# A hand-ordered attention and maxout kernel: its first part and its loop get new orders of loads, fillers, products and stores

## The chip, the cores and the metric

The kernel runs on one core of one Trainium2 chip. The metric is the device time of one execution in microseconds (us). Of the kernel before there are three timed runs and one profiled execution, and all numbers below are from those. Engines are called as in the profile: PE (TensorE), PEld (its weight loads), DVE (VectorE), ACT (ScalarE), POOL (GpSimd), SP (SyncE).

## What is computed

Eight batches of eight heads. For each head, `x` is 512 x 64 and `state` is 32 x 64:

```
a     = softmax(x @ state^T / 8)            # 512 x 32
xread = a @ state                           # 512 x 64
a2    = softmax(state @ x^T / 8)            # 32 x 512
sread = a2 @ x                              # 32 x 64
tok   = heads of [xread; sread] side by side  # (8 * 544) x 512
h     = max(tok @ w1, tok @ w2, tok @ w3)   # 4352 x 768
out   = h @ w_out                           # 4352 x 512, float32
```

## The kernel before, in words

Everything is fed to TensorE as bf16. The kernel never forms `xread`: since `xread @ W = a @ (state @ W)`, it first computes for each batch `G = state @ W`, a tile of 128 x 2 x 3 x 768 (`g_slice`, line 371, makes one slice of 128 columns of all three W; `g_run`, line 384, makes a run of up to 512 columns), and then the first layer is `aT` times `G` (`layer1`, line 417: 128 columns of the hidden layer for 512 tokens, three products of two matmuls each, one PSUM bank per product). The maximum of the three is taken in three steps: `max_first` (line 427, ACT copies the first product out of PSUM), `max_second` (line 432, DVE) and `max_third` (line 437, DVE, which writes `ht`). `layer2` (line 441) multiplies `ht` by `w_out`, six matmuls for one quarter of the batch's tokens, and `layer2_out` copies the result into `osb`, which is stored from there.

The attention weights `aT` take a chain of their own: `x` is transposed (`x_turn`, line 230, on PE for batches 0 and 1, by halves of the heads; `x_turn_dma`, line 246, by a transposing DMA on SP's queue for the others), `scores` (line 253, PE), `exps` (line 267, ACT), `sums` (line 272, DVE), `weights` (line 279, POOL or DVE) and a second transposition (`a_turn` on PE, `a_turn_dma` on SP's queue). The states are cast (`states_cast`), turned on PE (`states_turn`) and placed as a block diagonal (`states_place`). The state reads are small products (`sread`, line 314), scaled by DVE; `pad` (line 305) has POOL prepare a copy of `x` with ones for them from batch 2 on; their transposing DMA is `srt`, and `ap` puts the result in its place.

The order of the work is written out by hand, as three strings of short operations: FIRST (line 18) does batches 0 and 1 up to their hidden layers and starts batch 2; EACH (line 40) is performed for b = 2 to 6, its numbers being relative to b; LAST (line 48) ends the work. An operation such as `gc 1 0 A` names batch 1, slice 0 and the engine (A, D, P, S for ACT, DVE, POOL, SP). Every engine executes its own operations in the order of the text; semaphores hold an operation until its inputs are there and its buffer is free. Which of four single PSUM banks, or two pairs of banks, an operation gets is written out in the strings BANKS and PAIRS in the same order.

Loads of `x` (`lxg` for half of the heads of one batch, `lx` for all of them), of W (`lw m0 m1 i`: slices m0 to m1-1 of 128 columns of w1, w2 or w3 for i = 0, 1, 2) and of `w_out` (`lwo`) convert float32 to bf16 on their way and are issued by POOL into one queue, in order. The first half of batch 0 comes as float32 on SP's queue (`lxu`) and is cast by DVE (`cxu`). The states (`lst`) come by ACT's or SP's queue.

`busy n` (line 207) issues n matmuls of zeros; they compute nothing and are called fillers below. In FIRST there are 30 of them, all ahead of the first `layer1`.

Of the kernel before, what the change touches and what calls it, by code (L numbers as in the profile page):

```python
# [15 lines left out]


FIRST = """
    lxu 0 0 S; lst 0 A; lxg 1 0; zero; warm; clr 0; clr 1; clr 2; clr 3; stc 0 D; ident; busy 1;
    lst 1 S; busy 2; busy 1; busy 2; busy 1; busy 1; stt 0; busy 1; busy 2; cxu 0 0 D; stp 0 AD;  # L20
    stc 1 A; lxg 0 1; xt 0 0; lxg 1 1; lw 0 1 0; busy 1; lw 0 3 1; xtc 0 0 A; xt 1 0; xones 0; busy 2;
    busy 1; lw 0 2 2; xtc 1 0 DA; sc 0 0; xt 0 1; lw 1 2 0; busy 1; busy 1; lw 2 4 0; lw 2 4 2; sc 1 0;
    ex 0 0; ex 1 0; busy 1; xtc 0 1 A; xt 1 1; busy 1; busy 1; sum 0 0; busy 1; stt 1; lw 3 6 1; busy 1;
    sc 0 1; busy 1; ex 0 1; xtc 1 1 D; busy 1; sc 1 1; ex 1 1; busy 1; stp 1 A; lxg 2 1; wt 0 0 P;
    busy 1; xones 1; at 0 0; sum 1 0; busy 1; busy 1; sum 0 1; sr 0; busy 1; sum 1 1; g 0 0; wt 1 0 P;
    g 1 0; gc 1 0 A; wt 0 1 D; sr 1; busy 1; srs 0; lxg 2 0; at 0 1; at 1 0; wt 1 1 P; atc 0 0 D;
    at 1 1; gc 0 0 D; atc 0 1 A; lw 4 6 2; srs 1; atc 1 0 A; g 1 1; atc 1 1 D; gc 1 1 A; g 0 1;
    l1 0 0 1; g 1 2; m0 0 0; g 0 2; l1 1 0; gc 0 1 D; gc 1 2 A; l1 1 1; m0 1 0; ma 0 0; mb 0 0; ma 1 0;
    lw 4 6 0; mb 1 0; l1 0 1; g 0 3; m0 1 1; g 1 3; gc 0 2 A; l1 0 2; ma 1 1; l1 1 2; xtd 2; pad 2;
    m0 0 1; mb 1 1; ma 0 1; m0 0 2; lst 3 A; gc 0 3 DA; l1 0 3; m0 1 2; lwo; gc 1 3 A; ones; g 0 5;  # L30
    g 1 4; mb 0 1; ma 0 2; lxg 3 0; m0 0 3; mb 0 2; gc 0 5 A; lst 2 S; ma 1 2; l1 1 3; stc 3 P; m0 1 3;
    l1 0 5; mb 1 2; g 0 4; gc 1 4 A; g 1 5; ma 0 3; l1 1 4; m0 0 5; gc 0 4 A; mb 0 3; ma 1 3; m0 1 4;
    lxg 3 1; l1 0 4; sc 2 -; gc 1 5 A; xtd 3; mb 1 3; gr 2 1024 1280; m0 0 4; gr 2 1280 1792; ex 2 -;
    grc 2 1280 1792 A; l1 1 5; m0 1 5; ma 0 5; stc 2 A; mb 0 5; gr 2 512 1024; gr 2 1792 2304; sr 2;
    ma 1 4; mb 1 4; ma 0 4; mb 0 4; l2 0 3; grc 2 512 1024 A; stt 2; grc 2 1024 1280 D; gr 2 0 512;
    l2 0 0; l2 0 1; l2 0 2; grc 2 1792 2304 A; sum 2 -; l2c 0 0 A; grc 2 0 512 A; ma 1 5; wt 2 - P;
    srs 2; l2c 0 3 A; stp 2 A; mb 1 5; l2c 0 2 D; atd 2; so 0 2 4 P; stt 3; l2c 0 1 A; stp 3 DA;
    so 0 0 2 A; lx 4;
"""
EACH = """  # L40
    gr 1 0 512; gr 1 1792 2304; l2 -1 0; grc 1 0 512 D; l1 0 0; pad 1; srt -2; m0 0 0; sc 1 -; l2 -1 1;
    grc 1 1792 2304 A; ma 0 0; l2 -1 3; ex 1 -; gr 1 1024 1280; gr 1 512 1024; l2c -1 0 D;
    gr 1 1280 1792; sr 1; l2c -1 1 A; so -1 0 2 P; mb 0 0; l1 0 1; grc 1 1024 1280 A; l2c -1 3 A; xtd 2;
    m0 0 1; l1 0 2; m0 0 2; l1 0 3; sum 1 -; srs 1; grc 1 1280 1792 DA; ma 0 1; l1 0 5; mb 0 1; m0 0 3;
    ma 0 2; ap -2 A; wt 1 - P; mb 0 2; m0 0 5; l2 -1 2; ma 0 3; grc 1 512 1024 A; mb 0 3; l1 0 4;
    ma 0 5; mb 0 5; l2c -1 2 D; atd 1; m0 0 4; so -1 2 4 P; ma 0 4; lx 3; mb 0 4;
"""
LAST = """
    srt 6; l1 7 0; srt 7; l2 6 0; l1 7 2; m0 7 0; l1 7 3; l1 7 4; ap 7 D; m0 7 2; srt 5; ap 6 A; ma 7 0;
# [14 lines left out]
"""  # L64

BANKS = """
# [3 lines left out]
"""  # L70
PAIRS = """
    0110101010 1010101010 1001010010 1001010010 10
"""


# [601 lines left out]
```

## Time and profile before

| what | value |
|---|---|
| timed runs | 153.05, 153.10, 153.87 us (median 153.1) |
| profiled execution, its own time | 153.01 us |
| span of that profile | 151.2 us |
| PE busy | 146.6 us (97%) |
| DVE busy | 115.1 us (76%) |
| ACT busy | 85.4 us (56%) |
| POOL busy | 54.7 us (36%) |
| first row of `layer1` | starts 16.56 us from the span's start |

The span is the time between the first and the last instruction that the profile shows; the execution is 1.8 us longer. Busy time is counted per engine; the engines work side by side, so the shares don't add up. The chain of waits follows the work that ended last back from the end: at each step to what released it, or to the instruction ahead of it on the same engine. In its listing in order of time, each row has a start, a length, an engine and a line. All times are in us from the start of the span, unless ns is written.

### The profile page before, as it was taken

The page shows a single profiled execution, that of the slowest core. Times are in us where ns is not written, and L with a number is a line of the kernel's source. Part 1 is how long each engine was busy: PE and PEld are TensorE (multiplying, and loading weights), DVE is VectorE, ACT ScalarE, POOL GpSimd, SP SyncE. Part 2 cuts the span into 40 slices and gives each one's busy share as a digit, 9 for nine tenths or more (in the row PEclk, how much of TensorE's full clock was granted, in tenths as well). Part 3 has the DMA queues.
Part 4 walks back from the last instruction along what each step waited for, and adds up shares of the span by engine and source line. Part 5 has one row for each costly group of instructions (what it writes and reads, how often), then busy time and mean ns, then how long its engine had stood idle before and what let it go on. Part 6 is the DMA issues. An engine that isn't in the chain of part 4 may idle for free.

```text
span 151.2 us, 3644 instructions
## 1 busy us (share of the span) xinstructions
PE 146.6 (97%) x1434; PEld 73.6 (49%) x1434; DVE 115.1 (76%) x202; ACT 85.4 (56%) x147; POOL 54.7 (36%) x74
## 2 busy tenths in 40 slices
PE   6999999999999999999999999999999999999992
PEld 2465444344444443444354435443544445679771
DVE  6458899889168799879986998798879887675353
ACT  3567866779677671767175817581758353331220
POOL 6998518301336505460456054604260100001500
PEclk9999999999999999999999999999999999999999
DMA  3999999994919979998199829982133110300545
GB/s 112 241 193 195 198 196 203 161 197 59 204 53 262 225 89 269 152 193 182 60 168 228 174 94 163 206 176 80 72 139 87 68 79 7 131 8 17 188 170 198
DMA packets 38581, 22.30 MB, mean 147 GB/s; under 512 B 22032, under 2 KB 36368, under 8 KB 38560
## 3 DMA queue, kind: packets, MB, share of 16 engines
q0 software_dynamic: 15200, 13.44, 46.6%
q1 hardware_dynamic: 21920, 6.95, 23.5%
q10 hardware_dynamic: 1440, 1.64, 3.2%
q8 instruction: 12, 0.20, 0.5%
q14 instruction: 9, 0.07, 0.2%
HBM read 15.20 MB, written 8.91 MB: 159 GB/s over the span
## 4 chain that ended last, share of the span: by engine, by line
PE 92%; DMA 4%; issue 1%; POOL 1%; DVE 1%; POOLq 0%
PE pw L415 47%; PE po L446 25%; PE pg L362 6%; PE po L461 4%; DMA x<-in_x_dram 4%; PE psr L326 2%; PE ps L261 2%; PE idle L210 2%; PE pgh L362 1%; PE pat L294 1%; POOL x L169 1%; DVE held L521 0%; PE pt L221 0%; PE pxt L236 0%; PE idle L519 0%
## 5 line engine op out<-in xcount | busy, mean ns | idle before, releaser
L415 PE MATMUL pw<-aT,G 128*128 128x512 bf16 x288 | 66.6, 379 | 0.0
L430 ACT CAST t<-pw 128x512 bf16<-128x512 f32 (+1 forms) x54 | 30.4, 563 | 35.3 <-PE pw L415 21.6
L415 PEld LDWEIGHTS <-G 128*128 128x128 bf16 x288 | 27.2, 98 | 33.8 <-issue 2.4
L435 DVE TENSOR_TENSOR t<-t,pw 128x512 bf16<-128x512 bf16 (+1 forms) x54 | 35.3, 653 | 10.2 <-ACT t L430 7.7
L446 PE MATMUL po<-wout,ht 128*128 128x512 bf16 x168 | 39.8, 379 | 0.0
L439 DVE TENSOR_TENSOR ht<-t,pw 128x512 bf16<-128x512 bf16 x48 | 32.9, 685 | 4.1
L476 POOL DMA_DIRECT2D out_dram<-osb x12 | 6.9, 575 | 49.6 <-ACT t L430 20.4
L446 PEld LDWEIGHTS <-ht 128*128 128x128 bf16 x168 | 15.3, 98 | 19.2 <-issue 2.1
L283 POOL TENSOR_TENSOR a<-e,rden 128x1024 bf16<-128x1024 bf16 (+1 forms) x9 | 14.9, 1650 | 10.3 <-DVE rden L277 9.2
L402 ACT CAST G<-pg 128x1024 bf16<-128x1024 f32 (+1 forms) x19 | 17.1, 908 | 0.0
L310 POOL COPY xp<-x 128x1024 bf16<-128x1024 bf16 x12 | 12.3, 1065 | 5.0 <-DMA x<-in_x_dram 5.0
L453 DVE COPY osb<-po 128x512 f32<-128x512 f32 x14 | 9.6, 685 | 5.6 <-PE po L446 5.6
L453 ACT COPY osb<-po 128x512 f32<-128x512 f32 x15 | 8.9, 593 | 5.8 <-PE po L446 5.8
L210 PE MATMUL idle<-zero 128*128 128x512 bf16 x30 | 10.0, 436 | 1.3 <-DVE zero L188 1.3
L275 DVE TENSOR_REDUCE seen<-e 128x32 f32<-128x1024 bf16 (+1 forms) x10 | 10.0, 998 | 1.5 <-ACT e L268 1.5
L362 PE MATMUL pg<-w,bd 64*32 64x512 bf16 (+1 forms) x288 | 10.8, 362 | 0.0
L268 ACT ACTIVATE e<-ps 128x1024 bf16<-128x1024 f32 (+1 forms) x10 | 8.6, 861 | 2.1 <-PE ps L261 2.1
L402 DVE CAST G<-pg 128x1024 bf16<-128x1024 f32 (+1 forms) x10 | 9.5, 947 | 0.0
L471 POOL DMA_DIRECT2D out_dram<-osb x4 | 2.2, 542 | 19.9 <-ACT osb L465 19.9
L380 ACT CAST G<-pg 128x768 bf16<-128x768 f32 (+1 forms) x10 | 7.7, 774 | 2.1 <-PE pg L362 2.1
L415 PE MATMUL pw<-atp,w 128*128 128x256 bf16 x72 | 8.7, 272 | 0.0
L415 PEld LDWEIGHTS <-w 128*128 128x128 bf16 x72 | 6.9, 98 | 1.5
(71 smaller groups left out, 114.3 us busy)
## 6 DMA issues: line engine op xcount, KB each, us to landing
out_dram<-osb POOLq DMA_DIRECT2D x11, 512.0 KB, 3.1
x<-in_x_dram POOLq DMA_DIRECT2D x4, 512.0 KB, 6.6
x<-in_x_dram POOLq DMA_DIRECT2D x7, 256.0 KB, 8.4
w<-in_moe_w_dram POOLq DMA_DIRECT2D x5, 256.0 KB, 8.6
w<-in_moe_w_dram POOLq DMA_DIRECT2D x2, 384.0 KB, 8.8
wout<-in_moe_w_out_dram POOLq DMA_DIRECT2D x1, 768.0 KB, 9.5
out_dram<-osb SPq DMA_DIRECT2D x3, 256.0 KB, 2.3
osb<-in_x_dram SPq DMA_DIRECT2D x1, 512.0 KB, 4.0
```

The lines of the kernel that those rows point to most:

```text
L210: nc.tensor.matmul(p, zero[:, 0:128], zero, start=True, stop=True)
L275: nc.vector.reduce_sum(out=den, in_=parity(e[b], g), axis=AX.X)
L283: times[c](out=parity(a[b], g).rearrange("p j g s n -> p j (g s) n"), in0=parity(e[b], g).rearrange("p j g s n -> p j (g s) n"), in1=rdens ...
L310: nc.gpsimd.tensor_copy(out=xp[b][:, :, :, g * (D + 1):g * (D + 1) + D], in_=v[:, g])
L362: nc.tensor.matmul(p(s, g), bd(b, 2 * s + g)[64 * g:64 * g + 64, g, :], f(w_sb[64 * g:64 * g + 64, s]), start=True, stop=True, tile_positi ...
L402: copier[c[g]](out=v[:, g:h], in_=p[:, g:h, 0:c1 - c0])
L415: nc.tensor.matmul(pw[i][:, 0:n], lhs(i, k), rhs(k), start=(k == 0), stop=(k == nk - 1))
L430: nc.scalar.copy(out=t0s[b, m][:, 0:n], in_=open_ps["l", b, m][0][:, 0:n])
L435: nc.vector.tensor_max(t1s[b, m][:, 0:n], t0s.pop((b, m))[:, 0:n], open_ps["l", b, m][1][:, 0:n])
L439: nc.vector.tensor_max(ht[b][:, m, :], t1s.pop((b, m))[:, 0:n], open_ps.pop(("l", b, m))[2][:, 0:n])
L446: nc.tensor.matmul(p, ht[b][:, m, j * 128:(j + 1) * 128], wout_sb[:, m, :], start=(m == 0), stop=(m == NM - 1))
L453: copier[c[i]](out=o[:, j, i * w:i * w + w], in_=p[:, i * w:i * w + w])
```

## The change

Only the strings FIRST, EACH, BANKS and PAIRS differ; no function does, and LAST is the same text.

In FIRST:

- POOL sets the ones beside `x` first (`xones 0; xones 1`), and its queue then has batch 0's second half, both halves of batch 1, and W in twelve loads instead of nine: slices 0 and 1 of w2, slice 0 of w1, slice 0 and slice 1 of w3, slice 1 of w1, slice 2 of each, and the rest in five larger ones. Batch 2's `x` stands behind all of W (before: ahead of the last two W loads).
- The state loads 1 and 2 move from SP's queue to ACT's, load 1 from the very start to behind `xtc 1 1`; the cast of states 0 moves from DVE to ACT, those of 1 and 2 from ACT to POOL. The turning of states 1 (`stt 1`) moves from the middle of the attention of batch 1 to behind the fifth `layer1`.
- Batch 0's scores, sums and weights of both halves are finished ahead of batch 1's. The layers go `l1 0 0, 0 1, 0 2, 1 0, 1 1, 1 2, 0 3, 1 3, 0 5, 1 4, 0 4, 1 5` (before: `0 0, 1 0, 1 1, 0 1, 0 2, 1 2, 0 3, 1 3, 0 5, 1 4, 0 4, 1 5`).
- `lwo` is issued directly behind batch 2's `x`, and `pad 2`, which waits for that `x` on POOL, comes far later (before: `pad 2` ahead of `lwo`).
- At the end, batch 0's two stores both go by POOL's queue with the load of batch 4 between them (before: one by POOL's ahead of that load, the other by ACT's).
- 24 fillers instead of 30.

In EACH: the second `layer2` of the batch before moves ahead of the first `layer1`, the `g_run`s trade places in pairs, `srt` stands behind `xtd` on SP's queue, `ap` and the first store are last, and three evictions trade engines (`grc 1 1792 2304` from ACT to ACT and DVE, `grc 1 1280 1792` the other way, two `l2c` swap).

```diff
--- before
+++ after
 FIRST = """
-    lxu 0 0 S; lst 0 A; lxg 1 0; zero; warm; clr 0; clr 1; clr 2; clr 3; stc 0 D; ident; busy 1;
-    lst 1 S; busy 2; busy 1; busy 2; busy 1; busy 1; stt 0; busy 1; busy 2; cxu 0 0 D; stp 0 AD;
-    stc 1 A; lxg 0 1; xt 0 0; lxg 1 1; lw 0 1 0; busy 1; lw 0 3 1; xtc 0 0 A; xt 1 0; xones 0; busy 2;
-    busy 1; lw 0 2 2; xtc 1 0 DA; sc 0 0; xt 0 1; lw 1 2 0; busy 1; busy 1; lw 2 4 0; lw 2 4 2; sc 1 0;
-    ex 0 0; ex 1 0; busy 1; xtc 0 1 A; xt 1 1; busy 1; busy 1; sum 0 0; busy 1; stt 1; lw 3 6 1; busy 1;
-    sc 0 1; busy 1; ex 0 1; xtc 1 1 D; busy 1; sc 1 1; ex 1 1; busy 1; stp 1 A; lxg 2 1; wt 0 0 P;
-    busy 1; xones 1; at 0 0; sum 1 0; busy 1; busy 1; sum 0 1; sr 0; busy 1; sum 1 1; g 0 0; wt 1 0 P;
-    g 1 0; gc 1 0 A; wt 0 1 D; sr 1; busy 1; srs 0; lxg 2 0; at 0 1; at 1 0; wt 1 1 P; atc 0 0 D;
-    at 1 1; gc 0 0 D; atc 0 1 A; lw 4 6 2; srs 1; atc 1 0 A; g 1 1; atc 1 1 D; gc 1 1 A; g 0 1;
-    l1 0 0 1; g 1 2; m0 0 0; g 0 2; l1 1 0; gc 0 1 D; gc 1 2 A; l1 1 1; m0 1 0; ma 0 0; mb 0 0; ma 1 0;
-    lw 4 6 0; mb 1 0; l1 0 1; g 0 3; m0 1 1; g 1 3; gc 0 2 A; l1 0 2; ma 1 1; l1 1 2; xtd 2; pad 2;
...
+    lst 0 A; lxu 0 0 S; zero; clr 0; clr 1; clr 2; clr 3; warm; xones 0; busy 1; busy 1; busy 1;
+    xones 1; lxg 0 1; lxg 1 0; busy 1; stc 0 A; busy 1; busy 1; ident; busy 1; busy 1; busy 1;
+    cxu 0 0 D; lxg 1 1; busy 1; stt 0; xt 0 0; busy 1; xtc 0 0 D; lw 0 2 1; busy 1; stp 0 A; xt 0 1;
+    busy 1; lw 0 1 0; sc 0 0; ex 0 0; xt 1 0; busy 1; busy 1; busy 1; lw 0 1 2; lw 1 2 2; busy 1;
+    xtc 0 1 D; xtc 1 0 A; sc 0 1; xt 1 1; busy 1; sum 0 0; wt 0 0 D; ex 0 1; busy 1; busy 1; busy 1;
+    at 0 0; sc 1 0; lw 1 2 0; lw 2 3 2; lw 2 3 1; xtc 1 1 A; lw 2 3 0; busy 1; lst 1 A; ex 1 0; sum 0 1;
+    sum 1 0; busy 1; lw 3 6 2; sc 1 1; sr 0; wt 0 1 P; g 0 0; ex 1 1; g 1 0; wt 1 0 P; sr 1; at 0 1;
+    atc 0 0 A; busy 1; g 1 1; at 1 0; sum 1 1; gc 1 0 A; atc 0 1 D; lw 3 4 0; srs 1; g 0 1; wt 1 1 D;
+    atc 1 0 D; gc 0 0 A; lw 3 6 1; gc 1 1 A; l1 0 0; g 0 2; gc 0 1 A; m0 0 0; g 1 2; at 1 1; lw 4 6 0;
+    gc 0 2 A; lxg 2 1; stc 1 P; l1 0 1; m0 0 1; srs 0; l1 0 2; gc 1 2 A; lxg 2 0; ma 0 0; atc 1 1 D;
+    mb 0 0; l1 1 0; m0 0 2; lst 2 A; xtd 2; ma 0 1; mb 0 1; ma 0 2; l1 1 1; m0 1 0; m0 1 1; lwo; mb 0 2;
+    ma 1 0; g 1 3; g 0 3; stt 1; gc 1 3 A; stc 2 P; mb 1 0; l1 1 2; gc 0 3 A; g 0 4; lxg 3 0; ma 1 1;
...
+    mb 1 3; m0 0 5; ma 0 5; g 1 5; lst 3 A; gr 2 0 512; gc 1 5 A; l1 1 4 1; grc 2 0 512 DA; m0 1 4;
+    mb 0 5; ma 1 4; gr 2 1280 1792; gr 2 512 1024; grc 2 1280 1792 AD; ones; l1 0 4; stt 2; m0 0 4;
+    ma 0 4; mb 0 4; sc 2 -; stc 3 P; xtd 3; pad 2; mb 1 4; l2 0 3; stp 2 AD; l2 0 1; ex 2 -; sum 2 -;
...
 EACH = """
-    gr 1 0 512; gr 1 1792 2304; l2 -1 0; grc 1 0 512 D; l1 0 0; pad 1; srt -2; m0 0 0; sc 1 -; l2 -1 1;
-    grc 1 1792 2304 A; ma 0 0; l2 -1 3; ex 1 -; gr 1 1024 1280; gr 1 512 1024; l2c -1 0 D;
-    gr 1 1280 1792; sr 1; l2c -1 1 A; so -1 0 2 P; mb 0 0; l1 0 1; grc 1 1024 1280 A; l2c -1 3 A; xtd 2;
...
+    pad 1; gr 1 1792 2304; gr 1 0 512; grc 1 1792 2304 AD; l2 -1 0; l2 -1 1; l1 0 0; grc 1 0 512 D;
+    l2c -1 0 A; m0 0 0; sc 1 -; l2 -1 3; gr 1 1024 1280; ex 1 -; xtd 2; gr 1 1280 1792; l2c -1 1 D;
+    ma 0 0; gr 1 512 1024; mb 0 0; sr 1; grc 1 1024 1280 A; l1 0 1; l1 0 2; sum 1 -; l1 0 3; srs 1;
...
+    l1 0 4; so -1 2 4 P; m0 0 4; ma 0 4; lx 3; mb 0 4; atd 1; ap -2 A; so -1 0 2 P;
```

More of the change, by code (lines that the diff above doesn't have):

```diff
@@ L29 @@
-    lw 4 6 0; mb 1 0; l1 0 1; g 0 3; m0 1 1; g 1 3; gc 0 2 A; l1 0 2; ma 1 1; l1 1 2; xtd 2; pad 2;
[L30 to L38, printed above, removed]
+    lst 0 A; lxu 0 0 S; zero; clr 0; clr 1; clr 2; clr 3; warm; xones 0; busy 1; busy 1; busy 1;
@@ new lines @@
+    ma 1 0; g 1 3; g 0 3; stt 1; gc 1 3 A; stc 2 P; mb 1 0; l1 1 2; gc 0 3 A; g 0 4; lxg 3 0; ma 1 1;
+    m0 1 2; mb 1 1; stp 1 DA; ma 1 2; g 0 5; gc 0 5 D; lxg 3 1; mb 1 2; gc 0 4 A; l1 0 3; g 1 4;
+    gr 2 1792 2304; l1 1 3; m0 0 3; gc 1 4 A; m0 1 3; ma 0 3; l1 0 5; mb 0 3; grc 2 1792 2304 A; ma 1 3;
+    mb 1 3; m0 0 5; ma 0 5; g 1 5; lst 3 A; gr 2 0 512; gc 1 5 A; l1 1 4 1; grc 2 0 512 DA; m0 1 4;
+    mb 0 5; ma 1 4; gr 2 1280 1792; gr 2 512 1024; grc 2 1280 1792 AD; ones; l1 0 4; stt 2; m0 0 4;
@@ L39 @@
+    ma 0 4; mb 0 4; sc 2 -; stc 3 P; xtd 3; pad 2; mb 1 4; l2 0 3; stp 2 AD; l2 0 1; ex 2 -; sum 2 -;
+    l1 1 5; stt 3; l2c 0 1 D; l2 0 2; l2c 0 3 A; m0 1 5; ma 1 5; l2c 0 2 D; wt 2 - P; l2 0 0; stp 3 A;
+    mb 1 5; sr 2; gr 2 1024 1280; srs 2; l2c 0 0 D; so 0 0 2 P; lx 4; so 0 2 4 P; grc 2 512 1024 A;
+    atd 2; grc 2 1024 1280 D;
 """
 EACH = """
-    gr 1 0 512; gr 1 1792 2304; l2 -1 0; grc 1 0 512 D; l1 0 0; pad 1; srt -2; m0 0 0; sc 1 -; l2 -1 1;
-    grc 1 1792 2304 A; ma 0 0; l2 -1 3; ex 1 -; gr 1 1024 1280; gr 1 512 1024; l2c -1 0 D;
@@ L43 @@
-    gr 1 1280 1792; sr 1; l2c -1 1 A; so -1 0 2 P; mb 0 0; l1 0 1; grc 1 1024 1280 A; l2c -1 3 A; xtd 2;
-    m0 0 1; l1 0 2; m0 0 2; l1 0 3; sum 1 -; srs 1; grc 1 1280 1792 DA; ma 0 1; l1 0 5; mb 0 1; m0 0 3;
-    ma 0 2; ap -2 A; wt 1 - P; mb 0 2; m0 0 5; l2 -1 2; ma 0 3; grc 1 512 1024 A; mb 0 3; l1 0 4;
-    ma 0 5; mb 0 5; l2c -1 2 D; atd 1; m0 0 4; so -1 2 4 P; ma 0 4; lx 3; mb 0 4;
+    pad 1; gr 1 1792 2304; gr 1 0 512; grc 1 1792 2304 AD; l2 -1 0; l2 -1 1; l1 0 0; grc 1 0 512 D;
+    l2c -1 0 A; m0 0 0; sc 1 -; l2 -1 3; gr 1 1024 1280; ex 1 -; xtd 2; gr 1 1280 1792; l2c -1 1 D;
@@ L47 @@
+    ma 0 0; gr 1 512 1024; mb 0 0; sr 1; grc 1 1024 1280 A; l1 0 1; l1 0 2; sum 1 -; l1 0 3; srs 1;
+    l1 0 5; l2c -1 3 A; m0 0 1; m0 0 2; ma 0 1; mb 0 1; ma 0 2; m0 0 3; mb 0 2; srt -2; ma 0 3;
+    wt 1 - P; m0 0 5; mb 0 3; l2 -1 2; grc 1 1280 1792 A; grc 1 512 1024 A; ma 0 5; mb 0 5; l2c -1 2 D;
+    l1 0 4; so -1 2 4 P; m0 0 4; ma 0 4; lx 3; mb 0 4; atd 1; ap -2 A; so -1 0 2 P;
 """
@@ L66 @@
 BANKS = """
[3 rows of a table removed]
[3 rows of a table added]
 """
 PAIRS = """
-    0110101010 1010101010 1001010010 1001010010 10
+    0110101010 1010101101 0101010101 0101010101 01
 """
```

6 rows, old and new, of the table BANKS are left out of this document.

## The prediction

> **What bounds the kernel now.** First the page: busy time of each engine, and the span in forty slices.
>
> ```profile
> PE 146.6 (97%) x1434; PEld 73.6 (49%) x1434; DVE 115.1 (76%) x202; ACT 85.4 (56%) x147; POOL 54.7 (36%) x74
> ...
> PE   6999999999999999999999999999999999999992
> ```
>
> PE is busy in all slices but the first and the last. Some of it is fillers, so next comes the view of who waited for whom, for PE alone:
>
> ```profile
> PE idle L210 <- DVE zero L188: 1.3, 1, 1.3
> PE idle L519 <- DVE osb L465: 0.4, 1, 0.4
> PE pxt L236 <- DVE x L177: 0.2, 1, 0.2
> ```
>
> Only 0.2 us of waiting lies inside the run. An order of the same products can then gain only where PE does nothing useful, which is the start. Third, the chain of waits in order of time (start, length, what) shows that stretch:
>
> ```profile
> 3.58 5.97 DMA x<-in_x_dram
> ...
> 9.60 0.62 PE pxt L236 x8
> 10.22 0.65 PE idle L210 x3
> 10.87 0.22 PE pt L221 x4
> 11.09 0.22 PE idle L210
> 11.31 0.23 PE ps L261 x8
> 11.54 0.43 PE idle L210 x2
> 11.97 0.23 PE ps L261 x8
> 12.21 0.43 PE idle L210 x2
> 12.64 0.22 PE pat L294 x4
> 12.86 0.43 PE idle L210 x2
> 13.29 0.56 PE psr L326 x32
> 13.85 0.32 PE idle L210
> 14.18 0.45 PE pg L362 x16
> 14.62 0.56 PE psr L326 x32
> 15.19 0.32 PE idle L210
> 15.51 0.67 PE pat L294 x12
> 16.18 0.45 PE pg L362 x16
> 16.63 1.40 PE pw L415 x6
> ...
> 33.35 0.47 PE ps L261 x16
> ...
> 35.82 0.56 PE pg L362 x16
> ```
>
> The chain hangs on the last half of x of batches 0 and 1, which lands at 9.55. From then on PE is never idle, but 12 matmuls behind it are fillers: 0.65 + 0.22 + 3 x 0.43 + 2 x 0.32 = 2.80 us. From 16.63 all is work. So the time is: when the last x lands, plus the fillers and waits behind it, plus work that the change leaves the same (each product of before is in the new text once).
>
> **Fillers behind the last x: -1.3 us.** The new order also turns batch 1's second half (`xt 1 1`) last of the four. Ahead of it PE has done the same in both orders: states 0 turned, three halves turned, two half scores. Behind it the new text has 4 + 2 + 1 = 7 fillers, at 0.65 / 3 = 0.216 us each 1.51 us: 2.80 - 1.51 = 1.29 us less. Ahead of 9.55 stand 30 - 12 = 18 before and 24 - 7 = 17 now; there PE waits for x anyway. Turning states 1 (0.22) and one turning of `a` (0.22) also move behind the first `layer1`; they stay work, so the end gains nothing by them.
>
> The new steps, from rows above: `xt 1 1` 9.60 to 10.22; four fillers 11.08; `at 0 0` 11.30; `sc 1 0` 11.53; two fillers 11.96; `sc 1 1` 12.19; `sr 0` 12.75; `g 0 0` and `g 1 0` 13.20; `sr 1` 13.76; `at 0 1` 13.98, filler and turnover 14.30; `g 1 1`, `at 1 0`, `g 0 1` 14.95; then `l1 0 0`. Do the inputs keep up?
>
> ```profile
> L380 ACT CAST G<-pg 128x768 bf16<-128x768 f32 x9 | 7.3, 806 | 2.1 <-PE pg L362 2.1
> ...
> L283 POOL TENSOR_TENSOR a<-e,rden 128x512 bf16<-128x512 bf16 x3 | 3.4, 1135 | 0.6 <-DVE rden L277 0.6
> ...
> L275 DVE TENSOR_REDUCE seen<-e 128x16 f32<-128x512 bf16 x4 | 2.7, 669 | 1.5 <-ACT e L268 1.5
> ...
> L268 ACT ACTIVATE e<-ps 128x512 bf16<-128x512 f32 x4 | 2.4, 599 | 1.3 <-PE ps L261 1.3
> ...
> L297 ACT COPY aT<-pat 128x512 bf16<-128x512 bf16 x2 | 1.1, 588 | 0.3 <-PE pat L294 0.3
> L277 DVE RECIPROCAL rden<-seen 128x16 f32<-128x16 f32 x4 | 1.0, 253 | 0.1
> ...
> L197 POOL MEMSET x<- 128x64 bf16 x2 | 0.3, 170 | 0.0
> ```
>
> (Columns: count, busy us, mean ns; the lines by form.) The weights of batch 1's first half: 11.53 + 0.60 + 0.67 + 0.25 + 1.14 and a little between, about 14.25, for `at 1 0` at 14.5: in time by a quarter us. `G 0 0`: after `sc 1 1` at 12.19 ACT has an exponential (0.60), `atc 0 0` (0.59), `gc 1 0` (0.81) and `gc 0 0` (0.81), one behind the other, to 15.1: **late by about 0.2 us** for `l1 0 0`. I count +0.2, with bounds 0 and 0.5.
>
> **When the last x lands: -0.1.** Ahead of the x loads POOL now sets ones twice, 0.34 us at most. On the other side, state load 1 (128 KB) no longer runs beside them; at the rate of the next fence that is up to 0.66 us. Bounds -0.66 and +0.34; I take -0.1, near the middle.
>
> **W by slices: 0.** The busy time of each engine in two stretches, with DMA share and GB/s at the end:
>
> ```profile
> 10.00:22.00 12.00, 12.00 (x187) 6.25 (x185) 10.37 (x22) 9.05 (x15) 6.50 (x9) 1.00 1.43 198
> ...
> 44.90:60.15 15.25, 15.25 (x149) 6.82 (x148) 12.62 (x21) 8.86 (x15) 7.05 (x10) 1.00 0.95 210
> ```
>
> At 198 GB/s a load of 256 KB takes 1.32 us. Behind the last x at 9.55 stand `lw 0 2 1` and two single slices for `g 0 0`: 2.65 us, 12.2, wanted 12.75. Two more for `g 1 1`: 13.5, wanted 14.3. Three more for `g 0 2`: 15.5, wanted one `layer1` (1.40) behind 15.1, so 16.5. But a single slice may move slower. Before has one directly behind that x; its issue and its landing:
>
> ```profile
> 4.32 1.58 POOL L180 DMA_DIRECT2D w<-in_moe_w_dram  x2
> ```
>
> ```profile
> w<-in_moe_w_dram POOLq DMA_DIRECT2D x1, 128.0 KB, 6.0
> ```
>
> It lands at 10.32, 0.77 us behind the x, where the rate gives 0.66. With seven at 0.77, `g 0 2` has its slices at 9.55 + 1.32 + 5.39 = 16.26, still 0.2 early. So zero, but with little cover: each 0.1 us more on a slice costs up to 0.7 us less 0.2.
> The Trainium skill, "DMA: Bandwidth & Descriptors", Specifications, puts line rate at 512 B and more for a transfer and says that smaller ones are read, modified and written; a slice of 128 columns writes runs of 256 B. By that rule slices would go well below the rate and the change would lose; the 0.77 us above speaks for a small loss only.
>
> **w_out and batch 2's transposing transfer: 0.** Before, that transfer starts when batch 2's x lands:
>
> ```profile
> 22.13 3.34 SPq L248 DMA_TRANSPOSE xT<-x  x1
> ```
>
> ```profile
> wout<-in_moe_w_out_dram POOLq DMA_DIRECT2D x1, 768.0 KB, 9.5
> xT<-x SPq DMA_TRANSPOSE x1, 8.1
> ```
>
> It lands at 30.2, and its reader, the scores of batch 2 at 33.35, never waits. Now 512 KB of W come ahead of that x: 22.13 + 2.65 = 24.8, and 8.1 us later is 32.9 (33.4 with the slower slices). The scores now have four runs of G (0.28 each by the row at 35.82, which holds two) and one turning (0.22) ahead of them that stood behind: 33.35 - 1.1 + 1.3 = 33.55. So the 3.1 us of cover shrinks to 0.1 to 0.7, and I count nothing. w_out is issued right behind x instead of behind `pad 2`, which waits for that x. From 24.8 it takes 3.97 us at 198 GB/s, or at worst its 9.5 us of before, so it lands between 28.8 and 34.3; the first `layer2` stands behind the scores, at 34.0. I count zero, with 0.3 as the upper bound.
>
> **Banks and evictions: +0.1 in FIRST, 0 in the loop.** Four banks serve all single products, so a late eviction holds PE. Five `layer1` now follow with only one gap; DVE needs two steps of them each. No PE wait is seen before; I take +0.1, bounds 0 and 0.5. A round of the loop is 15.25 us, of which PE fills 15.25 and DVE 12.62. The same products stand in it; the half evictions that change engines go both ways, so no engine's sum moves. The cover is DVE's 2.6 us. Without it each 0.1 us of a round costs 0.5 us in five rounds. The load of batch b+3 keeps its place, and `srt` ahead of `atd` on SP has a whole `layer2` (1.29) more of cover, since the second one now stands ahead of the first `layer1`.
>
> **Sum.** -1.29 + 0.2 - 0.1 + 0.1 = -1.1. The profiled execution took 153.01 us (span 151.2, and 1.8 around it), the median of the runs is 153.1: the forecast is **151.9 us**, own range 151.2 to 152.3. A measurement of this kernel can tell about 0.5%, 0.77 us, from no change.
>
> **Rivals.**
>
> (1) *A slice of W costs as much as two* (1.32 us). For it: half of the run length, and the rule cited. Against it: the 0.77 us. `g 0 0` waits to 13.5 (0.8), `g 1 1` to 16.15 (1.1 more), `g 0 2` to 20.1 (1.8 more): +3.6, **155.5**. The loss at `g 0 2` is 7s - 5.6 us for a cost of s; from s = 0.96 the gain is gone, from 1.07 it is slower by over 0.5%. Half rate: 5%; in between (0.85 to 1.05, 152.3 to 153.5): 12%.
>
> (2) *Batch 2's transposing transfer waits for all of w_out* (3.97 us at 198 GB/s). It lands at 24.8 + 4.0 + 8.1 = 36.9, PE stands at the scores until then: +3.3, **155.2**, slower. It decides from 35.4 on. For it: the cover shrinks to some tenths, and the two already ran side by side with 8.1 and 9.5 us. Against it: before, it also had W and w_out beside it. 12%, half of that for a smaller delay near 153.8.
>
> (3) *The fillers stood for waits that come back*: ACT's row of four steps ends half a us later, or x lands 0.34 later. The gain falls to 0.3 to 0.6: **152.5**. 11%.
>
> (4) *The loop's new places cost 0.2 us in each of five rounds*: +1.0, **152.9**. Against it: unchanged sums of each engine. 5%.
>
> **How the numbers follow.** Forecast 55%, of which a few per cent lie below 151.2 (x early by its bound, no waits: 153.0 - 1.29 - 0.66 = 151.05). Rivals: (1) 17, (2) 12, (3) 11, (4) 5. Faster by over 0.5% (below 152.25) is the forecast and a little of (3): 0.57. Same: (3), (4), most of (1) in between: 0.25. Slower: (2), half rate: 0.18. For 8 in 10 the range runs from 151.0 to 153.8; half rate and the whole of (2) stay out.
>
> **What would show it.** The chain's `pw` row should start near 15.2 instead of 16.63, with seven fillers behind the turning at 9.6. PE's waits should show at most some tenths, at `pw` of batch 0 on ACT's G. A PE wait on a transfer at `pg` before 17 us is (1), at the scores of batch 2 near 33.5 is (2). A round of the loop should still be 15.25 us; if not, (4). The forecast is wrong if the first `pw` starts early and the end doesn't.

## The result: 0.8% slower, and the profile after

The changed kernel takes 1.008 times as long as the kernel before (95% interval 1.0052 to 1.0109), about 1.2 us more; the forecast was 1.1 us less, and the time lies above the range. It took 154.16 to 155.22 us (in run **a_again** 155.13 and 156.11), where before took 153.05 to 153.87; about half of its executions were 4 to 6 us longer still, at a lower granted clock of PE, and the comparisons leave these out. The profile below, from a_again, is of an execution of the unchanged new text that took 155.13 us, with a span of 153.3 us. It is one of the longer ones: against the profile of before it is 2.1 us longer, where the mean difference is 1.2 us. So the parts below are those of this profile and not of the mean.

Busy time, and PE and the DMA engines in forty slices, from its page:

```profile
PE 145.9 (95%) x1428; PEld 73.3 (48%) x1428; DVE 117.9 (77%) x205; ACT 84.5 (55%) x143; POOL 57.2 (37%) x79
...
PE   6789999994999999999999999999999999999992
...
DMA  4999999998635979899379838993603060210455
```

The tenth slice, 34.5 to 38.3 us, has a hole that before didn't have, and from 3.8 to 34.5 us the DMA engines are busy nine tenths or more. PE's waits name it (engine, line, what it waited for; total us, times, longest):

```profile
PE ps L261 <- DMA xT<-x: 2.1, 1, 2.1
...
PE pxt L236 <- DMA x<-in_x_dram: 1.2, 2, 0.9
```

`ps` on `xT` is the scores of batch 2 waiting for its transposing transfer. That one wait is as long as the whole difference of the two spans, 153.3 - 151.2 = 2.1 us. The second new wait, 1.2 instead of 0.2 us, is for `x` at the start. The chain in order of time now hangs on both:

```profile
2.33 6.75 DMA x<-in_x_dram
...
9.12 0.62 PE pxt L236 x8
9.74 0.86 PE idle L210 x4
10.61 0.23 PE ps L261 x8
10.84 0.45 PE pxt L236 x8
...
18.95 7.58 DMA x<-in_x_dram
...
26.55 10.67 DMA xT<-x
...
37.27 0.64 PE ps L261 x16
```

Before, PE itself was the chain from 9.60 us on. Now it runs through batch 2's `x`, which lands at 26.53, then through 10.67 us of the transposing transfer, and only at 37.27 back to PE. The order of time on PE at the start, from its timeline (start, length, engine, line, operation; in brackets the wait ahead of it):

```profile
7.81 0.62 PE L236 MATMUL pxt<-ident,x 128*128 128x128 bf16 x8 [0.94 <-DMA x<-in_x_dram]
9.12 0.62 PE L236 MATMUL pxt<-ident,x 128*128 128x128 bf16 x8 [0.25 <-DMA x<-in_x_dram]
10.68 0.61 PE L236 MATMUL pxt<-ident,x 128*128 128x128 bf16 x8
16.22 1.47 PE L415 MATMUL pw<-aT,G 128*128 128x512 bf16 x6
17.62 0.64 PE L362 MATMUL pg<-w,bd 64*32 64x384 bf16 x16
```

and the same of before, from the last turning on:

```profile
9.60 0.62 PE L236 MATMUL pxt<-ident,x 128*128 128x128 bf16 x8
...
16.56 1.47 PE L415 MATMUL pw<-aT,G 128*128 128x512 bf16 x6
17.96 0.52 PE L362 MATMUL pg<-w,bd 64*32 64x384 bf16 x16
```

So the 2.1 us of the two spans fall into: the last turning starts at 10.68 instead of 9.60 (+1.08); from there to the first `layer1` it is 5.54 instead of 6.96 us (-1.42); the wait at the scores (+2.12); and 0.3 us that are left. The -1.42 us are not all gain: one turning of `a` and the turning of states 1, 0.44 us of work by the rows in the prediction, moved behind the first `layer1` and come back in what is left. Counted so, the start gave nothing in this profile.

### The profile page after: what moved, and what is told of

The parts are those of the page before. It is cut to its first block, busy times and chain, and to the rows that moved or that the text cites. A ratio compares the mean times of both kernels' runs of the same rounds, so it can differ in the third digit from the quotient of the medians.

```text
span 158.8 us, 3616 instructions
## 1 busy us (share of the span) xinstructions
PE 147.2 (93%) x1415; PEld 74.6 (47%) x1428; DVE 117.9 (74%) x205; ACT 84.4 (53%) x143; POOL 57.3 (36%) x79
## 4 chain that ended last, share of the span: by engine, by line
PE 79%; DMA 14%; POOL 3%; issue 1%; DVE 1%; ACT 1%; DVEq 0%
PE pw L415 36%; PE po L446 24%; DMA xT<-x 9%; DMA x<-in_x_dram 6%; PE idle L210 5%; PE po L461 4%; PE pg L362 3%; PE ps L261 3%; PE psr L326 1%; POOL w L180 1%; PE pxt L236 1%; PE pgh L362 1%; POOL a L283 1%; POOL x L169 0%; DVE held L521 0%
## 5 line engine op out<-in xcount | busy, mean ns | idle before, releaser
L430 ACT CAST t<-pw 128x512 bf16<-128x512 f32 (+1 forms) x54 | 30.5, 564 | 29.5 <-PE pw L415 28.7
L415 PEld LDWEIGHTS <-G 128*128 128x128 bf16 x288 | 27.2, 98 | 33.1 <-issue 1.8
L283 POOL TENSOR_TENSOR a<-e,rden 128x1024 bf16<-128x1024 bf16 (+1 forms) x8 | 13.5, 1693 | 19.7 <-ACT osb L453 11.5
L476 POOL DMA_DIRECT2D out_dram<-osb x13 | 7.5, 575 | 32.8 <-ACT t L430 27.1
L402 ACT CAST G<-pg 128x1024 bf16<-128x1024 f32 (+1 forms) x19 | 15.9, 866 | 2.2 <-PE pg L362 2.0
L453 DVE COPY osb<-po 128x512 f32<-128x512 f32 x16 | 11.0, 687 | 4.4 <-PE po L446 4.4
L453 ACT COPY osb<-po 128x512 f32<-128x512 f32 x13 | 7.7, 593 | 9.3 <-PE po L446 9.3
L261 PE MATMUL ps<-bd,xT 128*128 128x64 bf16 x128 | 5.8, 199 | 5.4 <-DMA xT<-x 5.4
L402 DVE CAST G<-pg 128x512 bf16<-128x512 f32 (+1 forms) x12 | 10.5, 906 | 0.2 <-ACT G L402 0.2
L380 ACT CAST G<-pg 128x768 bf16<-128x768 f32 x11 | 8.4, 803 | 2.8 <-PE pg L362 2.7
L210 PE MATMUL idle<-zero 128*128 128x512 bf16 x24 | 8.6, 491 | 1.3 <-DVE zero L188 1.3
L180 POOL DMA_DIRECT2D w<-in_moe_w_dram x12 | 9.1, 772 | 1.1 <-DMA w<-in_moe_w_dram 0.7
L471 POOL DMA_DIRECT2D out_dram<-osb x4 | 2.2, 542 | 19.4 <-ACT osb L465 19.4
```

The source lines that it names most:

```text
L180: nc.gpsimd.dma_start(out=w_sb[:, :, i, m0 * 128:m1 * 128], in_=(moe_w1, moe_w2, moe_w3)[i].rearrange("(kk p) f -> p kk f", p=128)[:, :, m ...
L210: nc.tensor.matmul(p, zero[:, 0:128], zero, start=True, stop=True)
L283: times[c](out=parity(a[b], g).rearrange("p j g s n -> p j (g s) n"), in0=parity(e[b], g).rearrange("p j g s n -> p j (g s) n"), in1=rdens ...
L402: copier[c[g]](out=v[:, g:h], in_=p[:, g:h, 0:c1 - c0])
L415: nc.tensor.matmul(pw[i][:, 0:n], lhs(i, k), rhs(k), start=(k == 0), stop=(k == nk - 1))
L430: nc.scalar.copy(out=t0s[b, m][:, 0:n], in_=open_ps["l", b, m][0][:, 0:n])
```

## The experiments

All times are ratios to the kernel before on the same chip, with 95% intervals. The changed kernel stands at 1.008.

**a_again**: the changed kernel as it is.

> The changed kernel once more, as the base for the others and for a profile that PE's throttle did not disturb. Theory A (the transposing transfer of batch 2 is late, since it now runs beside w_out and batch 3's x, and PE stands at the scores of batch 2): a PE wait on xT of 1 us or more at about 34 us, and about 154.3 to 155 us. Theory B (W by slices is the whole loss): a PE wait at pg near 17 us of 1.2 us, none or only some tenths at the scores. Under both the first layer-one row starts near 15.4.

Its profile is the one above. The wait is at `sc 2`, and none is on W: theory A. The first `layer1` starts at 16.22, where both theories had 15.4, since `x` was late.

**b_wout_first**: the kernel before, with nothing moved but w_out's load.

```diff
-    ... l1 1 2; xtd 2; pad 2;
+    ... l1 1 2; lwo; xtd 2; pad 2;
-    ... m0 1 2; lwo; gc 1 3 A;
+    ... m0 1 2; gc 1 3 A;
```

> The kernel before with one part of the change alone: w_out is issued ahead of the padding of batch 2, so it is in the queue while batch 2's transposing transfer runs. Theory A: that transfer takes over 10 us instead of 8.1 and its 3 us of cover before the scores of batch 2 shrink to about 1 or are gone; 153.1 to 154.5. Theory B or no effect of w_out: it lands 8 us after its issue, 153.1.

1.0072 (1.0049 to 1.0095), 154.56 us. Nothing else of the order is changed (the first `layer1` starts at 16.85, before at 16.56), and this one move costs nearly what the whole change does. Waits, chain and the transfers' own times (size, us from issue to landing):

```profile
PE ps L261 <- DMA xT<-x: 1.2, 1, 1.2
```

```profile
22.22 12.55 DMA xT<-x
...
34.82 0.64 PE ps L261 x16
```

```profile
wout<-in_moe_w_out_dram POOLq DMA_DIRECT2D x1, 768.0 KB, 12.9
```

The transposing transfer is issued at 22.22, as in before (22.13), and takes 12.55 us instead of 8.1. w_out, issued at 17.23, lands at 30.1; the transposing transfer lands 4.6 us behind it, with half of batch 3's `x` (issued at 24.32, landed at 34.2) beside it.

**a_wout_late**: the changed kernel with `pad 2; lwo` in before's order.

```diff
-    ... m0 1 1; lwo; mb 0 2;
+    ... m0 1 1; pad 2; lwo; mb 0 2;
-    ... stc 3 P; xtd 3; pad 2; mb 1 4; ...
+    ... stc 3 P; xtd 3; mb 1 4; ...
```

> The changed kernel with w_out put back behind the padding of batch 2 (which waits for that batch's x), nothing else. Theory A1 (w_out in the queue is what slows the transposing transfer): the transfer lands 8 to 9 us after its issue at 26.5, so PE waits under 1 us at the scores, but w_out now lands 9 us behind 29, so PE waits 1 to 4 us at the first layer two instead: 154 to 157. Theory A2 (batch 3's x, or the late x of batch 2 alone, is what hurts): the transfer still takes over 10 us.

1.0136 (1.0114 to 1.0158), 155.13 us: slower than the changed kernel. The wait at the scores is gone, and another one is there:

```profile
PE po L446 <- DMA wout<-in_moe_w_out_dram: 2.2, 1, 2.2
```

```profile
18.44 7.69 DMA x<-in_x_dram
...
28.16 9.72 DMA wout<-in_moe_w_out_dram
```

```profile
xT<-x SPq DMA_TRANSPOSE x1, 4.4
```

With nothing of POOL's queue ahead of it the transposing transfer takes 4.4 us, where theory A1 had 8 to 9. But w_out now waits for batch 2's `x`, which lands at 26.1, and for `pad 2`, and lands at 37.9; the first `layer2` wants it at 35.7. With that `x` as late as this, one of the two is late in both orders that were tried.

**a_sc_late**: the changed kernel with `sc 2 -` behind two `layer2` of batch 0.

```diff
-    ma 0 4; mb 0 4; sc 2 -; stc 3 P; xtd 3; pad 2; mb 1 4; l2 0 3; stp 2 AD; l2 0 1; ex 2 -; sum 2 -;
+    ma 0 4; mb 0 4; stc 3 P; xtd 3; pad 2; mb 1 4; l2 0 3; stp 2 AD; l2 0 1; sc 2 -; ex 2 -; sum 2 -;
```

> The changed kernel with the scores of batch 2 placed behind two layer-two groups (2.6 us later on PE), nothing else. Theory A: most of the wait on xT is covered, up to 2.6 us come back: 152 to 153 us, and slow executions become rare. Theory B: no change, 154.3.

1.026 (1.0182 to 1.0338): both theories missed. PE no longer waits for `xT`, and yet the time rises. The exponentials and sums of batch 2 stand ahead of evictions on ACT and DVE and now start later, and PE waits for banks:

```profile
PE po L446 <- DVE osb L453: 1.0, 1, 1.0
PE pw L415 <- ACT osb L453: 0.8, 1, 0.8
```

Moving the reader away from the transfer was no free repair here.

**a_x3_late**: the changed kernel with batch 3's `x` behind `pad 2` and its transposing transfer behind `atd 2`.

```diff
-    ... gc 0 3 A; g 0 4; lxg 3 0; ma 1 1;
-    ... gc 0 5 D; lxg 3 1; mb 1 2; ...
+    ... gc 0 3 A; g 0 4; ma 1 1;
+    ... gc 0 5 D; mb 1 2; ...
-    ... stc 3 P; xtd 3; pad 2; mb 1 4; ...
+    ... stc 3 P; pad 2; lxg 3 0; lxg 3 1; mb 1 4; ...
-    atd 2; grc 2 1024 1280 D;
+    atd 2; xtd 3; grc 2 1024 1280 D;
```

> The changed kernel with batch 3's x loaded behind the padding of batch 2, so that only w_out stands beside batch 2's transposing transfer (and batch 3's transposing transfer behind the one of batch 2's weights on SP). Theory A2 (batch 3's x beside the transfer is what spreads it out): the transfer takes about 8 us, the wait at the scores falls under 1 us, slow executions vanish, 153 to 153.8. Theory A1: it still takes 10 us or more and PE waits about 2 us, 154.5.

1.0046 (1.0018 to 1.0074), 153.8 us. The transposing transfer of batch 2 was issued at 27.19 and took

```profile
xT<-x SPq DMA_TRANSPOSE x1, 6.7
```

instead of 10.7, beside the end of w_out and no other load of POOL's (w_out was issued at 20.03 and took 11.1 us). So in the changed kernel both are in its way: w_out, and the 512 KB of batch 3's `x` that POOL issues from 0.14 us behind it on (at 26.69). This profile is of an execution of 159.62 us, the longest of the eleven, in which PE also waits 4.3 us for the transposing transfer of batch 3; but a_x3p below, which makes the same move, has 6.1 us for the transfer of batch 2 in an execution of 156.38 us. The time itself is not clear of that of the changed kernel: the two intervals overlap.

**b_x2_late**: the kernel before with batch 2's `x` behind the last two loads of W, as in the change.

```diff
-    ... stp 1 A; lxg 2 1; wt 0 0 P; ... srs 0; lxg 2 0; at 0 1; ...
+    ... stp 1 A; wt 0 0 P; ... srs 0; at 0 1; ...
-    lw 4 6 0; mb 1 0; ...
+    lw 4 6 0; lxg 2 1; lxg 2 0; mb 1 0; ...
```

> The kernel before with one other part of the change alone: batch 2's x behind the last two W loads (512 KB), w_out still behind the padding. Theory A1: the transfer starts 2.7 us later and takes no longer, w_out lands near 36 us just in time, 153.1 to 153.6. Theory A3 (the late x alone uses up the cover): a PE wait at the scores of 0 to 1 us.

1.0156 (1.0119 to 1.0192): both theories missed. Again 4.4 us for the transposing transfer, and no wait at the scores of batch 2. The loss comes later: batch 3's `x` is late as well, its `xtd 3` holds SP's queue until 39.77, and the transposing of batch 2's weights stands behind it:

```profile
PE pw L415 <- DMA aT<-a: 1.4, 1, 1.4
```

**b_fewer**: the kernel before without five of its 12 fillers behind the last turning, so seven as in the change. `busy 0` draws its bank and issues nothing.

```diff
-    ... xt 1 1; busy 1; busy 1; sum 0 0; busy 1; stt 1; lw 3 6 1; busy 1;
+    ... xt 1 1; busy 1; busy 0; sum 0 0; busy 0; stt 1; lw 3 6 1; busy 0;
-    busy 1; xones 1; at 0 0; sum 1 0; busy 1; busy 1; sum 0 1; sr 0; ...
+    busy 0; xones 1; at 0 0; sum 1 0; busy 1; busy 0; sum 0 1; sr 0; ...
```

> The kernel before with five of the 12 fillers behind the last turning of x left out (three ahead of the half scores of batch 0, one ahead of at 0 0, one ahead of sr 0); products, transfers and their places are those of before. It takes the first term of the forecast by itself. Forecast's theory (fillers behind the last x are pure cost): 5 x 0.216 = 1.08 us less, the first pw row near 15.5, 152.2. Rival (the fillers stand for waits that come back: the exponentials, the sums and the weights behind them set the time): waits of 0.5 to 1.1 us at pat, psr or pw, 152.8 to 153.3. If the forecast's theory holds here, the first term was right and the changed kernel loses it elsewhere.

0.9999 (0.9977 to 1.0021): nothing. PE's timeline, from the last turning to the first `layer1`:

```profile
9.96 0.61 PE L236 MATMUL pxt<-ident,x 128*128 128x128 bf16 x8
...
11.50 0.41 PE L261 MATMUL ps<-bd,xT 128*128 128x64 bf16 x8 [0.49 <-ACT xT L243]
...
16.86 1.47 PE L415 MATMUL pw<-aT,G 128*128 128x512 bf16 x6
```

From 9.96 to 16.86 it is 6.90 us, with 12 fillers 6.96. The five fillers were 1.08 us; 1.02 of it came back as waits, half of it at the half scores behind ACT's copy of `xT`. Here the rival won outright: in before's order the fillers stood for waits.

**a_pieces**: the changed kernel with W in ten larger loads instead of twelve. (The twelve are eight of 128 KB, two of 256 KB and two of 384 KB; behind slice 2 of each stand four, not five, and one of these is a single slice.)

```diff
-    ... lw 0 1 2; lw 1 2 2; ... lw 2 3 2; lw 2 3 1; ... lw 2 3 0; ... lw 3 6 2; ... lw 3 4 0; ... lw 3 6 1; ... lw 4 6 0;
+    ... lw 0 2 2; ... lw 2 4 2; lw 2 4 1; ... lw 2 4 0; ... lw 4 6 2; ... lw 4 6 1; ... lw 4 6 0;
```

> The changed kernel with W in ten loads of mostly 256 KB instead of twelve, in nearly the same order. Theory B: the slices cost by their number, the last W and batch 2's x land about 0.7 us earlier and the wait at pg near 17 us shrinks. Theory A: the wait at the scores shrinks by the same 0.7 us at most, 153.6 to 154.3.

1.0098 (1.0067 to 1.0129): no better than the change. Busy times of each engine in stretches (the last column is GB/s), first of a_again, then of a_pieces:

```profile
11.00:15.00 4.00, 4.00 (x116) 2.71 (x113) 2.84 (x7) 3.67 (x6) 2.86 (x4) 1.00 1.81 179
```

```profile
11.00:15.00 4.00, 3.88 (x117) 2.49 (x115) 2.78 (x8) 3.51 (x6) 2.40 (x3) 1.00 1.49 203
```

The larger pieces move faster here, 203 against 179 GB/s. But v1 and v2 below, with the small loads, have 192 GB/s in this stretch, and a_x3p, with the larger ones, 192 too, so the size isn't shown to be the reason. The larger pieces put more bytes ahead of the slice that is wanted next, and PE stands at slice 2 of G:

```profile
18.38 0.62 PE L362 MATMUL pg<-w,bd 64*32 64x384 bf16 x16 [1.24 <-DMA w<-in_moe_w_dram]
```

The wait at the scores is gone in this run: the transposing transfer was issued at 25.18 and landed at 33.5. The 1.2 us at W stand in its place.

**a_x3p**: a_pieces and a_x3_late together (the edits of both).

> The changed kernel with batch 3's x and its transposing transfer behind pad 2 and atd 2 (as in a_x3_late) and W in ten larger loads (as in a_pieces) together. Theory (the loss of the change is the slow transposing transfer of batch 2 beside w_out and batch 3's x, plus the W slices): the two savings add, 1.3 + 0.5 us off the changed kernel, about 153.2 to 153.5, no PE wait at the scores of batch 2, some tenths at pg of g 0 2. Rival (both save the same wait, at the scores of batch 2): about 153.8 to 154.2, like a_x3_late alone. Below 152.5 only if the shorter start then reaches the end whole.

1.0208 (1.0162 to 1.0254): both theories missed, by 2 to 3 us.

```profile
PE ps L261 <- DMA xT<-x: 1.4, 1, 1.4
...
PE pg L362 <- issue: 1.2, 1, 1.2
```

The scores that wait are now those of batch 3, whose transposing transfer, issued at 44.17, takes 6.45 us beside the load of batch 4 and a store; the 1.2 us are at slice 2 of G again (it starts at 19.24, 0.1 us behind the landing of its last load of W). My 0.5 us for the larger pieces had no ground, since a_pieces itself had shown none.

**v1**: the changed kernel with batch 2's `x` ahead of the last 512 KB of W, w_out behind `pad 2`, and `g 0 4`, `g 0 5` later.

```diff
-    ... gc 0 0 A; lw 3 6 1; gc 1 1 A; ... at 1 1; lw 4 6 0; gc 0 2 A; lxg 2 1; ... lxg 2 0; ... lwo; ... pad 2; ...
+    ... gc 0 0 A; lw 3 4 1; lxg 2 1; lxg 2 0; gc 1 1 A; ... at 1 1; lw 4 6 1; lw 4 6 0; gc 0 2 A; ... pad 2; lwo; ...
-    ... gc 0 3 A; g 0 4; lxg 3 0; ... g 0 5; gc 0 5 D; ... gc 0 4 A; l1 0 3; g 1 4; ...
+    ... gc 0 3 A; lxg 3 0; ... l1 0 3; g 0 4; g 0 5; gc 0 5 D; gc 0 4 A; l1 1 3; g 1 4; ...
```

> A version: the changed kernel's first part, but batch 2's x ahead of the last four slices of w2 and w1 (as before), w_out behind the padding, and two runs of G for batch 0 one layer later so that W has time. Theory A in any form: the transfer lands near 31 us, no wait at the scores, the gain of the shorter start shows: 152 to 153. If the start gains nothing: 153.3 or more.

1.0216 (1.0184 to 1.0247). The transfers did as expected (`xT` issued at 22.8 and landed at 30.2, no wait for it), but the moved runs of G left two `layer1` without the gap between them:

```profile
PE pw L415 <- ACT t L430: 2.7, 3, 1.2
```

**v2**: v1 with all runs of G where the change has them (the first two lines of the edit above alone).

> The changed kernel with batch 2's x ahead of the last 512 KB of W, and w_out and pad 2 in before's order (pad 2, then w_out); unlike v1 every run of G keeps its place. Theory (the start of the changed kernel is good for 0.4 to 1.4 us, and its loss is batch 2's transposing transfer that meets w_out): that transfer starts near 22.8 as in v1 and is alone, w_out is issued near 24.8, no PE wait at the scores of batch 2, none of v1's 2.7 us at pw on ACT; 152.3 to 153.0, below both kernels if x comes in time. Rival (the late W costs what the early x saves): a PE wait of 0.5 to 1.5 us at pg of the fourth to the sixth slice of G on W, 153.5 to 154.5. Second rival (the scores of batch 2 and its evictions, in the changed kernel's order, cost about half a us at po on DVE by themselves): 153.3.

1.0043 (1.002 to 1.0067), 154.0 us: the first rival of its expectation. No wait at the scores, none at `w_out`; but

```profile
PE pg L362 <- DMA w<-in_moe_w_dram: 1.5, 2, 1.1
```

```profile
15.11 1.47 PE L415 MATMUL pw<-aT,G 128*128 128x512 bf16 x6
17.66 0.52 PE L362 MATMUL pg<-w,bd 64*32 64x384 bf16 x16 [1.08 <-DMA w<-in_moe_w_dram]
```

The first `layer1` starts 1.45 us earlier than before, of which 0.44 us is the work that moved behind it, and 1.5 us go into waiting for W. No version that was tried beats the kernel before.

## Why the prediction was wrong, point by point

**W_out and batch 2's transposing transfer: 0.** This is the step that failed, by 2.1 us. It took 8.1 us for the transfer wherever it stands, and against rival (2), that it waits for w_out, it said that before it "also had W and w_out beside it". The runs show that the length depends on what POOL's queue moves at the time. The view of the DMA queues, by stretches, tells when the data of the transfer moved: 2048 packets, 0.52 MB, in SP's queue (q1; q0 is POOL's and q10 ACT's; each row has packets, MB, and the packets' time as a share of the 16 engines'). In a_wout_late from 27.4 to 30.1 us (with 32 closing packets of next to no data), and in before from 23.4 to 26.6 us:

```profile
q1 hardware_dynamic: 2080, 0.52, 104.0%
```

```profile
q1 hardware_dynamic: 2048, 0.52, 101.9%
q0 software_dynamic: 121, 0.06, 13.2%
```

| kernel | issued | its data moved | landed | POOL's queue meanwhile |
|---|---|---|---|---|
| a_wout_late | 26.1 | 27.4 to 30.1 | 30.5 | nothing; w_out from 30.2 |
| b_x2_late | 25.3 | 26.6 to 29.2 | 29.7 | nothing; w_out from 29.3 |
| before | 22.1 | 23.4 to 26.6 | 30.2 | the end of W, landed at 24.8; w_out from 26.7 |
| v2 | 23.8 | 25.1 to 27.7 | 30.4 | the end of W, landed at 26.2; w_out from 27.7 |
| a_pieces | 25.2 | 27.7 to 30.8 | 33.5 | w_out to 28.9, then batch 3's `x` |
| a_x3_late | 27.2 | 29.2 to 32.5 | 33.9 | w_out to 30.6 |
| b_wout_first | 22.2 | 26.2 to 34.2 | 34.8 | W, w_out to 29.7, half of batch 3's `x` |
| changed (a_again) | 26.55 | 28.7 to 35.7 | 37.2 | w_out to 30.0, batch 3's `x` |

With POOL's queue empty, the first data move 1.3 us behind the issue, they take 2.6 us, and the transfer lands 0.5 us later: 4.4 us. In before, the data began after 1.3 us as well and were through at 26.6, yet the transfer landed only at 30.2. What was left by then were its closing packets, and they moved beside w_out. v2 shows these alone, from 27.8 to 30.4 us:

```profile
q0 software_dynamic: 225, 0.23, 99.3%
q1 hardware_dynamic: 32, 0.00, 1.7%
```

From the last data to the landing it is 0.5 us in a_wout_late and b_x2_late, where w_out's data begin behind the closing packets, and 2.7 to 5.1 us in before, b_fewer, v1 and v2, where they run beside them. So some 3 us of before's 8.1 were already w_out's, at the tail of the transfer. When w_out is queued ahead, the transfer's beginning waits too. In b_wout_first, from the issue at 22.22 to 26.2 us, only POOL's queue moved:

```profile
q0 software_dynamic: 1080, 0.81, 132.7%
```

In the changed kernel the first data come 2.1 us behind the issue, they take 7.0 us beside the end of w_out and batch 3's `x`, and the landing follows 1.5 us later. The length decided, not the late `x` alone: PE came to the scores at 35.15 and not at the predicted 33.55 (the start had given nothing, and the two turnings that had moved stood ahead of the scores too), so that 8.1 us behind the `x` at 26.53 would have been in time.

This is the direction of rival (2), given 12% with 155.2 us; it put the landing at 36.9, where the profile has 37.2. That nearness is luck. The `x` landed at 26.53, not at 24.8, 10.7 us follow, not 12.1, and part of the delay was batch 3's `x`, which the rival doesn't have: without it the transfer took 6.7 (a_x3_late) and 6.1 us (a_x3p). The Trainium skill, "DMA: Bandwidth & Descriptors", Queues, rings and completion order, says that each DMA engine takes turns between queues packet by packet. Read as an even share, which is an estimate, the transfer of b_wout_first would end about twice 4.4 us behind its issue, at 31.0; the measured 34.8, and the 4.0 us without a packet of it, speak against an even share. What in the chip holds it back isn't shown by any run, only the times.

**Fillers behind the last x: -1.3.** Right for the new text: 5.54 us from the last turning to the first `layer1`, predicted 5.55 with the 0.2 us for G, before 6.96 (v2: from 9.56 to 15.11, 5.55 too). Of the 1.42 us between them 0.44 is the work that moved, so that 1.0 us is gain. The reason given was only half of it: b_fewer shows that leaving out fillers alone, in before's order, gains nothing. That the new order also finishes batch 0 first, so that the inputs are there, is the likely other half; no run tries it alone.

**G of batch 0 late: +0.2.** Together with the fillers it gives the measured 5.54 us; PE's waits name none on G, so it isn't seen apart.

**When the last x lands: -0.1.** Wrong in kind, and +1.08 in this profile. The prediction had PE wait for the last of the four halves, with the fillers ahead of it free. In the new order PE waits for the second and third (0.94 and 0.25 us in a_again), and from the third turning to the last one it is 1.54 to 1.56 us in every run of it, four fillers among them. So the last turning starts 1.55 us behind the third one, which starts about as the third half lands: at 9.56 (v2), 9.58 (v1), 9.93 (a_pieces), 10.68, 11.02 (a_x3_late) in different runs. In before's order it starts between 9.60 and 9.96 (b_fewer). The halves land as the transfers' rate has it; the two stretches of before, and then of a_again, with GB/s at the end:

```profile
5.00:7.00 2.00, 1.67 (x19) 0.89 (x17) 1.29 (x2) 1.64 (x3) 2.00 (x5) 1.00 1.45 194
7.00:9.00 2.00, 2.00 (x32) 1.41 (x30) 0.56 (x2) 1.41 (x3) 2.00 (x4) 1.00 1.45 186
```

```profile
5.00:7.00 2.00, 1.87 (x16) 1.01 (x14) 1.18 (x2) 0.96 (x2) 2.00 (x4) 1.00 1.31 155
7.00:9.00 2.00, 1.07 (x17) 0.83 (x17) 0.70 (x2) 0.28 (x2) 1.93 (x3) 1.00 1.33 169
```

In v2 they are 187 and 191 GB/s, and there `x` was in time. Why the rate differs between runs that have the same text up to there stays open.

**W by slices: 0.** The price of a slice was not the trouble, so rival (1) is out as a mechanism: in a_again four single slices landed one behind the other between 11.75 and 14.69 us, 0.74 us each, where the prediction had 0.77. But the cover of 0.2 us was not there. Where the first `layer1` starts early (15.11 in v2), slice 2 of G waits until 17.66; where it starts at 16.22 (a_again), slice 2 starts at 17.62 without a wait. Predicted were slices at 16.26. W comes when it comes, whatever PE gains ahead of it: against before's 17.96, only 0.3 us of the start's gain is left there in both, less than the 0.44 us of work that moved. The prediction counted its bytes from 9.55 on at 198 GB/s; the stretches above and the 179 GB/s of 11 to 15 us are what it got.

**Banks: +0.1, loop: 0.** The 0.3 us that are left over are less than the 0.44 us of work that moved, so no loss at the banks is seen. A round of the loop takes 15.25 us as before, so rival (4) is out. Rival (3) was right about before's fillers, and x landed late by more than its 0.34 us; that took the gain of the start in this profile, but the loss came with the wait at the scores.

So the price: about 2.1 us at the scores, against a start that gave nothing in this profile, its 1.0 us being taken up by the late `x`. Sum of the terms as measured: +1.08 - 1.42 + 2.12 + 0.3 = 2.1. Of the 3.2 us between this and the forecast of -1.1, 2.1 are the wait at the scores and most of the rest is the late `x`, which v2 did not have; v2 waited for W instead.

## What to carry to other kernels

A transfer's length in a profile holds what the other queues moved at the time, from its first packet to its landing: before something is moved, list what its queue and its neighbours' queues will hold at the new time, and take the length without them as the base (4.4 us here, not 8.1). Where the DMA engines are busy nine tenths or more from beginning to end, as from 3.8 to 34.5 us here, a shorter product order turned into a wait for the next bytes (1.2 us in a_pieces, 1.5 in v2); the order of the loads has to bring the gain. A filler that covers a wait costs nothing, so leave it out alone, as an experiment, before its time is counted as gain.

## What the runs showed of the hardware

POOL's issue of a load also waits, for the landing of the load eight places ahead of it. From POOL's timeline in a_again:

```profile
9.36 0.75 POOL L180 DMA_DIRECT2D w<-in_moe_w_dram  x1 [0.44 <-DMA x<-in_x_dram]
10.71 0.74 POOL L180 DMA_DIRECT2D w<-in_moe_w_dram  x1 [0.60 <-DMA x<-in_x_dram]
12.04 0.74 POOL L180 DMA_DIRECT2D w<-in_moe_w_dram  x1 [0.59 <-DMA w<-in_moe_w_dram]
```

The three loads eight places ahead landed at 9.08, 10.42 and 11.75, each some 0.3 us before. In a_pieces, where most loads are twice as large, it is the same: the eleventh load is issued at 9.98, 0.28 us behind the landing of the third. So the number of loads under way, eight, sets it, and not their size. The strings don't ask for that. The trace counts the landings of POOL's loads on eight semaphores in turn, so the limit may be the program's own and not the chip's; no run tells which. More and smaller loads reach it sooner, and whatever else POOL has to do (here a half of the weights `a`) stands behind it.

Between 11 and 15 us, runs of 256 B (single slices) moved at 179 to 192 GB/s in six kernels, and pieces twice as wide at 192 and 203 GB/s in two. The Trainium skill, "DMA: Bandwidth & Descriptors", Specifications, has line rate from 512 B on; the direction agrees, but the ranges touch, and a loss near a half is not there.
